# Second engines for four elementwise operations in a list-scheduled attention and feed-forward kernel

## The chip, the cores and the metric

The kernel runs on one core of a Trainium2 chip. The metric is the device time of one execution in microseconds. The engines are called as in the profile: PE is TensorE (matmul), PEld its weight loads, DVE is VectorE, ACT is ScalarE, POOL is GpSimd and SP is SyncE, which issues the DMAs.

## What is computed

Sliding-window attention with a few always visible first keys (sinks), and behind it a feed-forward layer with ELU (batch 4, 8 heads, 768 positions, head dimension 64; 3072 tokens, model width 512, hidden width 2048):

```python
scores = (1 / sqrt(64)) * q @ k.T
keep = (pos_k < n_sink) | ((0 <= pos_q - pos_k) & (pos_q - pos_k < window))   # n_sink 4, window 128
a = softmax(where(keep, scores, -1e9))
x = (a @ v) laid out as 3072 x 512
h = x @ w_in
out = where(h > 0, h, exp(min(h, 0)) - 1) @ w_out
```

Inputs are float32, the two weights float64.

## The kernel before

The 24 tiles of 128 tokens are cut into nine chunks (three of two tiles, six of three). For each chunk `attention` handles four pairs of heads, tile by tile, and `feed_forward` runs over 16 blocks f of 128 hidden units. The first two chunks' blocks come in halves (chunk 0 first half, chunk 1 first half, then the second halves), since meanwhile the 32 weight pieces are still being loaded and converted.

Matmuls run on 16-bit parts (or rounded 32-bit ones for the scores): a value is split into a high half and a low half (value minus high half), and products of the halves are summed in PSUM. So most of the elementwise work makes halves:

- weights (`weights`, `weight_f32`): per piece L292 (ACT), L293 and L294 (DVE, 16-bit shift and mask), L295 (DVE) give a float32 piece wv; L442 (ACT) its high half, L443 (POOL) its low half.
- keys and queries (`split_keys`): L508 (ACT) high, L512 and L514 (POOL) low.
- values (`vtile`): L531 (ACT) high half of V, L532 (DVE) low half, both from the loaded tile vs.
- probabilities, per tile and head: scores (L577, L578; in the first two chunks L584), mask and minimum (L603, DVE), exp (L605, ACT), reciprocal (L609, L610), then L617 (ACT) the scaled high half of probabilities, L618 (DVE) the low half, and for the sinks three small POOL operations (L624, L627, L628). A DMA transpose on the SP queue (L636) turns pq into pt, the values matmul (L650, L655) follows, and L687 (ACT), L688 (DVE) make the halves of x.
- hidden units, per block: 12 matmuls into h (L715); L723 (ACT) g = exp; L725 (DVE) g = (g - 1) times a scale; L726 (DVE) the ELU, max(min(g, 0), h), with h from PSUM, which also frees h's bank; L728 (ACT) the high half gh, L729 (POOL) the low half gl; then the matmuls into acc (L736).

The order is made at build time by `Plan`. Each step is a task with an engine, a duration in us, and dependencies; buffers are rings (`RINGS`), and a writer depends on the users of the buffer some turns earlier. A due time for each task is worked out backward from the matmuls, and a forward pass places tasks: the engine that can start earliest takes its ready task with the earliest due time. A task may have a second way (`or_`: engine, duration, function); it then stands in both engines' queues, and the one that reaches it first takes it:

```python
else:
    while later[e] and later[e][0][0] <= s:
        _, n, t = heapq.heappop(later[e])
        heapq.heappush(now[e], (t.due, n, t))
    ...
    t.take(e)
dur = t.dur
if e == "DVE" and t.slow > 1.0:
    both = min(max(free["POOL"] - s, 0.0), dur * t.slow)
    dur += both * (1.0 - 1.0 / t.slow)
```

With equal start times the engine named first in the order PE, ACT, DVE, POOL, SP takes the task. `slow` stretches a task's planned time on DVE while POOL is planned as busy. Passes backward and forward are repeated eight times, the best modelled end is kept, and every engine then runs its instructions in exactly that order (`keep_order`). No task of the kernel before has a second way.

Of the kernel before, what the change touches and what calls it, by code (L numbers as in the profile page):

```python
# [273 lines left out]
def pool_us(n):  # L274
    return 0.25 + 0.0019 * n
# [73 lines left out]
def fast_path(tc, ctx, first, kq, vx, wt, out, nw, flag):  # L349
# [129 lines left out]
    def attention(c):  # L479
# [12 lines left out]
        def split_keys(h):  # L492


            st = kqs[slot("kqs")]
            buf = kqr[slot("kq")] if c >= WHOLE else None
            o, kw = KQ_OFF[c, h], kc + qc
            if c < WHOLE:
                ld = None
                if (c, h) not in first["kq"]:  # L500
                    ld = add("SP", 0.4, lambda: nc.sync.dma_start(st[:, :kw], kq[:, o : o + kw]), lat=dma_us(P * kw * 4) * 1.15)
                users = []
                return st, None, ld, ld, users
            raw, hi = st[:, :kw], buf[:, :kw]
            ld = None
            if (c, h) not in first["kq"]:
                ld = add("SP", 0.4, lambda: nc.sync.dma_start(raw, kq[:, o : o + kw]), lat=dma_us(P * kw * 4) * 1.15)
            th = add("ACT", act_us(kw), lambda: nc.scalar.activation(hi, raw, AF.Copy), deps=[ld])  # L508

            def low():  # L510
                n = kc if c >= DUP else kw
                nc.gpsimd.tensor_tensor(buf[:, KQ_MAX : KQ_MAX + n] if c >= DUP else buf[:, kw : 2 * kw], raw[:, :n], hi[:, :n].bitcast(F32), ALU.subtract)  # L512
                if c >= DUP:
                    nc.gpsimd.tensor_tensor(hi[D:, kc:], raw[D:, kc:], hi[D:, kc:].bitcast(F32), ALU.subtract)  # L514

            tl = add("POOL", pool_us(kc) + pool_us(qc) if c >= DUP else pool_us(kw), low, deps=[th])
            users = []
            ring("kqs", [ld or th], [th, tl])
            ring("kq", [th], users)
            lo = buf[:, KQ_MAX : KQ_MAX + kc] if c >= DUP else buf[:, kw : 2 * kw]  # L520
            return hi, lo, th, tl, users

        def vtile(g):

            if g not in v_of:
                st, i = vs[slot("vs")], slot("vt")
                ld = None
                if g not in first["vs_"]:
                    ld = add("SP", 0.4, lambda: nc.sync.dma_start(st, vx[:, g * VT : (g + 1) * VT]), lat=dma_us(P * VT * 4))
                hi, lo, users = vh[i], vl[i], []  # L530
                va = add("ACT", act_us(VT), lambda: nc.scalar.activation(hi, st, AF.Copy, scale=V_SCALE), deps=[ld])  # L531
                vb = add("DVE", 0.13 + 0.00108 * VT, lambda: nc.vector.scalar_tensor_tensor(lo, st, V_SCALE, hi, ALU.mult, ALU.subtract), deps=[va], slow=1.35)  # L532
                ring("vs", [ld or va], [va, vb])
                ring("vt", [va], users)
                v_of[g] = hi, lo, va, vb, users
            return v_of[g]

        def sink_rows(b):

            if b not in sk_of:  # L540
                st, sk, users = vs[slot("vs")], sks[slot("sk")], []
                o = SINKS + b * VT
                ld = add("SP", 0.4, lambda: nc.sync.dma_start(st, vx[:, o : o + VT]), lat=dma_us(P * VT * 4))
                va = add("ACT", act_us(VT), lambda: nc.scalar.activation(sk, st, AF.Copy, scale=V_SCALE), deps=[ld])
                vb = add("DVE", 0.13 + 0.00108 * VT, lambda: nc.vector.scalar_tensor_tensor(sk[64:96, :], st[64:96, :], V_SCALE, sk[64:96, :], ALU.mult, ALU.subtract), deps=[va])
                ring("vs", [ld], [va, vb])
                ring("sk", [va], users)
                sk_of[b] = sk, vb, users
            return sk_of[b]

        k = 0
        for p in range(NP):
# [5 lines left out]
            for g in ts:  # L558
# [53 lines left out]
                for e in range(2):  # L612
                    src = e3[:, e, :wd].rearrange("p (b k) -> p b k", k=KW)[:, :, NS:]
                    hi = pq[:, 2 * e * nb : (2 * e + 1) * nb, :]
                    lo = pq[:, (2 * e + 1) * nb : (2 * e + 2) * nb, :]
                    re = rs[:, e : e + 1]
                    a = add("ACT", act_us(nb * P, True), lambda src=src, hi=hi, re=re: nc.scalar.activation(hi, src, AF.Copy, scale=re), deps=[rr])  # L617
                    b = add("DVE", 0.478 if nb == 2 else 0.33, lambda src=src, hi=hi, lo=lo, re=re: nc.vector.scalar_tensor_tensor(lo, src, re, hi, ALU.mult, ALU.subtract), deps=[a], slow=1.5)  # L618
                    parts += [a, b]
                    his.append(a)  # L620
                if t >= 2:

                    def sinks(e3=e3, rs=rs, tmp=tmp, pq=pq):
                        nc.gpsimd.tensor_tensor(tmp, e3[:, :, 0:NS], rs.unsqueeze(2).to_broadcast([P, 2, NS]), ALU.mult)  # L624
                        hi = pq[:, 8, 0:96].rearrange("p (g r) -> p g r", g=3)[:, :, 0 : 2 * NS]
                        flat = tmp.rearrange("p e k -> p (e k)")
                        nc.gpsimd.tensor_copy(hi[:, 0:3:2, :], flat.unsqueeze(1).to_broadcast([P, 2, 2 * NS]))  # L627
                        nc.gpsimd.tensor_tensor(hi[:, 1, :], flat, hi[:, 0, :], ALU.subtract)  # L628

                    b = add("POOL", 0.75, sinks, deps=[rr])  # L630
                    parts.append(b)
                    his.append(b)
                ring("e", [r for r, _ in exps], parts)
# [64 lines left out]
    def feed_forward(c, f0, f1, start):  # L698
# [4 lines left out]
        for f in range(f0, f1):  # L703
            hp = h_ps[slot("h")]
            gf = gs[slot("g")][:, :n]
            i = slot("gh")
            gh, gl = ghs[i], gls[i]

            def stage1(hp=hp, f=f):
                win = w[2 * f].rearrange("p t (a f) -> p t a f", a=ND)  # L710
                k = 0
                for d in range(ND):
                    xh, xl = x[d][:2]
                    for part, xx in ((0, xh), (1, xh), (0, xl)):
                        nc.tensor.matmul(hp[:, :n], win[:, part, d, :], xx[:, :n], start=k == 0, stop=k == 3 * ND - 1)  # L715
                        k += 1

            s1 = add("PE", 12 * (n / 2400 + 0.002), stage1, deps=[v for d in x for v in d[2:4]] + list(w_done[2 * f]), pos=start + 2 * (f - f0))
            for d in x:
                d[4].append(s1)  # L720

            sums = es_of[:, c * NF + f : c * NF + f + 1]
            a = add("ACT", act_us(n) + 0.18, lambda gf=gf, hp=hp, sums=sums: nc.scalar.activation(gf, hp[:, :n], AF.Exp, scale=1.0 / G_SCALE, accum_out=sums), deps=[s1])  # L723
            exps_done.append(a)
            b = add("DVE", 0.14 + 0.00057 * n, lambda gf=gf: nc.vector.tensor_scalar(gf, gf, -1.0, G_SCALE, ALU.add, ALU.mult), deps=[a], slow=2.1)  # L725
            b = add("DVE", dve_us(n), lambda gf=gf, hp=hp: nc.vector.scalar_tensor_tensor(gf, gf, 0.0, hp[:, :n], ALU.min, ALU.max), deps=[b])  # L726
            ring("h", [s1], [b])
            th = add("ACT", act_us(n), lambda gf=gf, gh=gh: nc.scalar.activation(gh[:, :n], gf, AF.Copy), deps=[b])  # L728
            tl = add("POOL", pool_us(n), lambda gl=gl, gf=gf, gh=gh: nc.gpsimd.tensor_tensor(gl[:, :n], gf, gh[:, :n], ALU.subtract), deps=[th])  # L729

            def stage2(order, gl=gl, gh=gh, f=f):
                def run():
                    wout = w[2 * f + 1]
                    for k, i in order:
                        gg, part = ((gh, 0), (gh, 1), (gl, 0))[k]
                        nc.tensor.matmul(acc[i], gg[:, i * P : (i + 1) * P], wout[:, part, :], start=f == f0 and k == 0, stop=f == f1 - 1 and k == 2)  # L736
                return run

            deps = [th, tl, *w_done[2 * f + 1], *(evacs[:nt] if f == f0 else [])]
            at2 = start + 2 * (f - f0) + 1 + 2 * LAG  # L740
            if f < f1 - 1:
                s2 = [add("PE", 3 * nt * 0.215, stage2([(k, i) for k in range(3) for i in range(nt)]), deps=deps, pos=at2)]
            else:

                s2 = [add("PE", 3 * 0.215, stage2([(k, i) for k in range(3)]), deps=deps, pos=at2 + 0.01 * i) for i in range(nt)]
            ring("g", [a], [th, tl])
            ring("gh", [th], s2)
# [307 lines left out]
```

## Time and profile before

| | |
|---|---|
| median of three runs | 658.54 us (656.51 to 658.79) |
| profiled execution, its own time | 656.69 us |
| its span, first to last instruction | 654.8 us |
| mean granted TensorE clock | 0.986 of full speed |
| busy: PE, DVE, ACT, POOL | 610.5, 460.8, 441.8, 332.6 us |

Spans and busy times are those of the one profiled execution. Busy is the time in which at least one instruction of an engine was running. Matmuls overlap in the engine and their ends are modelled, so a busy PE need not be PE at its peak. A time given to an instruction contains what it waited for inside the engine after its start.

### The profile page before, as it was taken

The numbers are of one execution on the slowest core, as the hardware profiler recorded it, in microseconds if no ns is written. First come the engines' busy times: TensorE is split into PE (matmuls) and PEld (weight loads), VectorE is DVE, ScalarE is ACT, GpSimd is POOL, SyncE is SP. The second block draws the span as 40 slices with busy tenths as digits, with TensorE's granted clock in tenths as the row PEclk, the third lists the DMA queues.
The fourth block names the chain that finished last, engine by engine and source line by source line (L and its number), as shares of the span: only waits on it lengthen the run. The fifth ranks groups of instructions, "written<-read, shape, count | busy, mean of one in ns | idle before, by whom it ended". The sixth has DMA issues, their size and how long they took to land.

```text
span 654.8 us, 13359 instructions
## 1 busy us (share of the span) xinstructions
PE 610.5 (93%) x4449; PEld 369.6 (56%) x4449; DVE 460.8 (70%) x1243; ACT 441.8 (67%) x1300; POOL 332.6 (51%) x497
## 2 busy tenths in 40 slices
PE   3786799699999999999999999999999999999995
PEld 1453466466776565655555555565555556555552
DVE  6989979987866777568677877668677776533222
ACT  4988778878877777667667776677667766523231
POOL 0166968795656665535445655544445654212221
PEclk9998889999999999999999999999999999999998
DMA  7889974766746554346444766565654733301001
GB/s 280 212 214 305 259 239 161 222 167 171 190 110 132 148 149 108 90 125 180 123 105 95 197 150 124 78 145 140 145 101 102 200 84 90 75 27 48 1 0 54
DMA packets 125500, 90.78 MB, mean 139 GB/s; under 512 B 104304, under 2 KB 104304, under 8 KB 125424
## 3 DMA queue, kind: packets, MB, share of 16 engines
q1 hardware_dynamic: 125424, 89.85, 52.9%
q8 instruction: 37, 0.61, 0.4%
q14 instruction: 39, 0.32, 0.1%
HBM read 57.32 MB, written 7.34 MB: 99 GB/s over the span
## 4 chain that ended last, share of the span: by engine, by line
PE 80%; DVE 8%; issue 4%; POOL 3%; ACT 2%; DMA 2%; SPq 0%; DVEq 0%; POOLq 0%; ACTq 0%
PE h L715 35%; PE acc L736 34%; PE po L650 4%; PE s L577 3%; PE s L578 3%; DVE wv L295 2%; POOL w L443 1%; DVE wu L294 1%; DMA pt<-pq 1%; DVE wu L293 1%; DVE e L603 1%; POOL gl L729 1%; DVE pq L618 1%; POOL kq L512 1%; PE s L584 1%
## 5 line engine op out<-in xcount | busy, mean ns | idle before, releaser
L715 PE MATMUL h<-x,w 128*128 128x384 f16 (+1 forms) x1728 | 278.4, 312 | 7.4 <-DVE g L726 5.6
L715 PEld LDWEIGHTS <-w 128*128 128x128 f16 x1728 | 166.4, 99 | 102.2 <-issue 4.9
L729 POOL TENSOR_TENSOR gl<-g,gh 128x384 f16<-128x384 f32 (+1 forms) x144 | 128.2, 891 | 179.7 <-ACT gh L728 145.6
L736 PE MATMUL acc<-w,gh 128*128 128x512 f16 x768 | 193.4, 381 | 0.0
L725 DVE TENSOR_SCALAR g<-g 128x384 f32<-128x384 f32 (+1 forms) x144 | 70.5, 489 | 104.9 <-ACT g L723 104.3
L723 ACT ACTIVATE g<-h 128x384 f32<-128x384 f32 (+1 forms) x144 | 65.2, 453 | 98.3 <-PE h L715 90.3
L618 DVE SCALAR_TENSOR_TENSOR pq<-e,st,pq 128x256 f16<-128x256 f32 (+1 forms) x192 | 111.3, 611 | 16.0 <-ACT pq L617 15.1
L736 PEld LDWEIGHTS <-gh 128*128 128x128 f16 x768 | 70.3, 98 | 69.7 <-issue 1.1
L736 PE MATMUL acc<-w,gl 128*128 128x512 f16 x384 | 109.2, 379 | 0.1
L603 DVE CUSTOM_DVE_ANT_0 e<-s,m 128x264 f32<-128x264 f32 (+1 forms) x192 | 71.7, 404 | 46.5 <-PE s L578 40.8
L605 ACT ACTIVATE e<-e,st 128x264 f32<-128x264 f32 (+1 forms) x192 | 93.1, 486 | 9.5 <-DVE st L603 8.6
L617 ACT ACTIVATE pq<-e,st 128x256 f16<-128x256 f32 (+1 forms) x192 | 85.0, 480 | 15.8 <-DVE st L610 13.6
L728 ACT ACTIVATE gh<-g 128x384 f16<-128x384 f32 (+1 forms) x144 | 69.3, 481 | 34.7 <-DVE g L726 33.3
L512 POOL TENSOR_TENSOR kq<-kqs,kq 128x396 fp32r<-128x396 f32 (+1 forms) x56 | 67.7, 1209 | 38.0 <-ACT kq L508 37.8
L726 DVE SCALAR_TENSOR_TENSOR g<-g,h 128x384 f32<-128x384 f32 (+1 forms) x144 | 72.7, 505 | 1.5
L736 PEld LDWEIGHTS <-gl 128*128 128x128 f16 x384 | 37.6, 98 | 45.9 <-POOL gl L729 0.6
L508 ACT ACTIVATE kq<-kqs 128x780 fp32r<-128x780 f32 (+2 forms) x56 | 49.0, 878 | 20.2 <-PE s L578 16.8
L577 PE MATMUL s<-kq 128*128 128x264 f32 x160 | 55.2, 363 | 6.1 <-DVE st L603 2.9
L443 POOL TENSOR_TENSOR w<-wv,w 128x512 f16<-128x512 f32 x32 | 38.8, 1215 | 39.4 <-ACT w L442 25.7
L514 POOL TENSOR_TENSOR kq<-kqs,kq 64x384 fp32r<-64x384 f32 (+1 forms) x56 | 55.7, 995 | 4.4
L650 PE MATMUL po<-pt,vh 128*64 128x128 f16 x704 | 42.0, 231 | 8.4 <-DMA pt<-pq 6.7
L650 PEld LDWEIGHTS <-vh 128*64 128x64 f16 x704 | 30.1, 115 | 22.5 <-issue 16.0
(79 smaller groups left out, 604.1 us busy)
## 6 DMA issues: line engine op xcount, KB each, us to landing
raw<-in_wt_dram SPq DMA_DIRECT2D x32, 512.0 KB, 5.6
kqs<-in_kq_dram SPq DMA_DIRECT2D x24, 456.0 KB, 3.5
kqs<-in_kq_dram SPq DMA_DIRECT2D x24, 390.0 KB, 3.7
vs<-in_vx_dram SPq DMA_DIRECT2D x28, 256.0 KB, 3.1
out_dram<-wv SPq DMA_DIRECT2D x24, 256.0 KB, 3.6
vm<-in_vx_dram SPq DMA_DIRECT2D x6, 768.0 KB, 4.8
kqs<-in_kq_dram SPq DMA_DIRECT2D x12, 326.0 KB, 3.6
pt<-pq SPq DMA_TRANSPOSE x96, 3.2
```

The lines of the kernel that those rows point to most:

```text
L512: nc.gpsimd.tensor_tensor(buf[:, KQ_MAX : KQ_MAX + n] if c >= DUP else buf[:, kw : 2 * kw], raw[:, :n], hi[:, :n].bitcast(F32), ALU.subtract)
L577: nc.tensor.matmul(sp[:, :wd], q, hi[:, c0 : c0 + wd], start=True, stop=False)
L603: red = add("DVE", 0.24 + 0.001 * wd, lambda ee=ee, me=me, sp=sps[e], m=m, wd=wd: nc.vector.tensor_tensor_reduce(ee, sp[:, :wd], m[:, :wd] ...
L605: ex = add("ACT", 0.47 + 0.00085 * wd, lambda ee=ee, me=me, rs=rs[:, e : e + 1]: nc.scalar.activation(ee, ee, AF.Exp, bias=me, scale=-1.0, ...
L617: a = add("ACT", act_us(nb * P, True), lambda src=src, hi=hi, re=re: nc.scalar.activation(hi, src, AF.Copy, scale=re), deps=[rr])
L618: b = add("DVE", 0.478 if nb == 2 else 0.33, lambda src=src, hi=hi, lo=lo, re=re: nc.vector.scalar_tensor_tensor(lo, src, re, hi, ALU.mult ...
L650: nc.tensor.matmul(po[e * D : (e + 1) * D, oc], vts[i][x][:, vo : vo + D], pt[:, (2 * e + part) * nb + i, :], start=new, stop=last)
L715: nc.tensor.matmul(hp[:, :n], win[:, part, d, :], xx[:, :n], start=k == 0, stop=k == 3 * ND - 1)
L725: b = add("DVE", 0.14 + 0.00057 * n, lambda gf=gf: nc.vector.tensor_scalar(gf, gf, -1.0, G_SCALE, ALU.add, ALU.mult), deps=[a], slow=2.1)
L726: b = add("DVE", dve_us(n), lambda gf=gf, hp=hp: nc.vector.scalar_tensor_tensor(gf, gf, 0.0, hp[:, :n], ALU.min, ALU.max), deps=[b])
L729: tl = add("POOL", pool_us(n), lambda gl=gl, gf=gf, gh=gh: nc.gpsimd.tensor_tensor(gl[:, :n], gf, gh[:, :n], ALU.subtract), deps=[th])
L736: nc.tensor.matmul(acc[i], gg[:, i * P : (i + 1) * P], wout[:, part, :], start=f == f0 and k == 0, stop=f == f1 - 1 and k == 2)
```

## The change

Four tasks get a second way: the ELU's exp - 1 step (L725) may run on POOL, the low half of V (L532) may run on POOL as two operations (scale, then subtract), the scaled high half of probabilities (L617) may run on POOL, and the high half of g (L728) may run on DVE. Three planned durations are raised (low half of the keys by 1.12, the sinks from 0.75 to 1.0, and the stretch of V's low half from 1.35 to 1.5). A function `low` is also defined in `sink_rows`, where nothing uses it.

```diff
-            tl = add("POOL", pool_us(kc) + pool_us(qc) if c >= DUP else pool_us(kw), low, deps=[th])
+            tl = add("POOL", 1.12 * (pool_us(kc) + pool_us(qc)) if c >= DUP else pool_us(kw), low, deps=[th])
...
-                vb = add("DVE", 0.13 + 0.00108 * VT, lambda: nc.vector.scalar_tensor_tensor(lo, st, V_SCALE, hi, ALU.mult, ALU.subtract), deps=[va], slow=1.35)
+                def low():
+                    nc.gpsimd.tensor_scalar(st, st, V_SCALE, None, ALU.mult)
+                    nc.gpsimd.tensor_tensor(lo, st, hi, ALU.subtract)
+
+                vb = add("DVE", 0.13 + 0.00108 * VT, lambda: nc.vector.scalar_tensor_tensor(lo, st, V_SCALE, hi, ALU.mult, ALU.subtract), deps=[va], slow=1.5, or_=("POOL", 1.95, low))
...
-                    a = add("ACT", act_us(nb * P, True), lambda src=src, hi=hi, re=re: nc.scalar.activation(hi, src, AF.Copy, scale=re), deps=[rr])
+                    a = add("ACT", act_us(nb * P, True), lambda src=src, hi=hi, re=re: nc.scalar.activation(hi, src, AF.Copy, scale=re), deps=[rr], or_=("POOL", 0.25 + 0.00088 * nb * P, lambda src=src, hi=hi, re=re: nc.gpsimd.tensor_scalar(hi, src, re, None, ALU.mult)))
...
-                    b = add("POOL", 0.75, sinks, deps=[rr])
+                    b = add("POOL", 1.0, sinks, deps=[rr])
...
-            b = add("DVE", 0.14 + 0.00057 * n, lambda gf=gf: nc.vector.tensor_scalar(gf, gf, -1.0, G_SCALE, ALU.add, ALU.mult), deps=[a], slow=2.1)
+            b = add("DVE", 0.14 + 0.00057 * n, lambda gf=gf: nc.vector.tensor_scalar(gf, gf, -1.0, G_SCALE, ALU.add, ALU.mult), deps=[a], slow=2.1, or_=("POOL", 0.25 + 0.00088 * n, lambda gf=gf: nc.gpsimd.tensor_scalar(gf, gf, -1.0, G_SCALE, ALU.add, ALU.mult)))
...
-            th = add("ACT", act_us(n), lambda gf=gf, gh=gh: nc.scalar.activation(gh[:, :n], gf, AF.Copy), deps=[b])
+            th = add("ACT", act_us(n), lambda gf=gf, gh=gh: nc.scalar.activation(gh[:, :n], gf, AF.Copy), deps=[b], slow=2.1, or_=("DVE", 0.14 + 0.00057 * n, lambda gf=gf, gh=gh: nc.vector.tensor_copy(gh[:, :n], gf)))
```

## Rows read from the trace of the kernel before

**Rows 1.** The page: TensorE's busy tenths in 40 equal slices of the span.

```profile
PE   3786799699999999999999999999999999999995
```

**Rows 2.** Stretches: us, busy us per engine (instructions), granted clock, DMA share, GB/s.

```profile
16.00:49.00 33.00, 25.73 (x174) 16.12 (x175) 29.55 (x103) 28.98 (x92) 12.62 (x21) 1.00 0.87 213
...
49.00:98.00 49.00, 37.38 (x316) 24.26 (x314) 44.66 (x102) 39.79 (x112) 35.25 (x50) 0.86 0.94 268
...
98.00:131.00 33.00, 27.94 (x209) 18.56 (x207) 33.00 (x66) 27.62 (x72) 25.21 (x31) 1.00 0.61 193
...
16.00:131.00 115.00, 91.06 (x695) 58.94 (x696) 107.21 (x269) 96.38 (x275) 73.08 (x100) 0.94 0.82 231
...
180.00:620.00 440.00, 438.99 (x3197) 260.20 (x3196) 293.69 (x783) 290.30 (x853) 216.59 (x323) 1.00 0.47 114
```

**Rows 3.** Groups, 16 to 131 us, VectorE: busy us, mean ns | idle before.

```profile
L293 DVE TENSOR_SCALAR wu<-raw 128x512 uint16<-128x512 uint16 x30 | 21.7, 722 | 0.0
...
L295 DVE SCALAR_TENSOR_TENSOR wv<-acc,wu 128x512 int32<-128x512 int32 x30 | 20.4, 681 | 1.2 <-ACT acc L292 1.0
...
L294 DVE TENSOR_SCALAR wu<-raw 128x512 uint16<-128x512 uint16 x30 | 19.9, 664 | 0.0
...
L618 DVE SCALAR_TENSOR_TENSOR pq<-e,st,pq 128x256 f16<-128x256 f32 x31 | 16.2, 550 | 1.6 <-ACT pq L617 1.3
...
L725 DVE TENSOR_SCALAR g<-g 128x256 f32<-128x256 f32 x21 | 11.1, 528 | 4.3 <-ACT g L723 4.3
...
L726 DVE SCALAR_TENSOR_TENSOR g<-g,h 128x256 f32<-128x256 f32 x21 | 8.5, 406 | 0.0
...
L532 DVE SCALAR_TENSOR_TENSOR vl<-vs,vh 128x512 f16<-128x512 f32 x4 | 4.1, 1042 | 0.0
```

**Rows 4.** Groups, 16 to 131 us, GpSimd.

```profile
L443 POOL TENSOR_TENSOR w<-wv,w 128x512 f16<-128x512 f32 x30 | 36.2, 1208 | 39.0 <-ACT w L442 25.3 <-DVE x L688 10.1 <-DVE g L726 1.9
```

**Rows 5.** The chain of waits, 98 to 131 us, shares by line.

```profile
by line: issue 23.6%; DVE wv L295 14.7%; POOL w L443 12.1%; DVE wu L294 11.4%; DVE wu L293 9.9%; DVE g L725 7.5%; DVE pq L618 5.2%; POOL gl L729 4.6%; ACT w L442 3.5%; DVE g L726 3.0%; ACT acc L292 2.1%; DVE e L603 2.1%; ACT g L723 1.4%; DV
```

**Rows 6.** In order of time: start us, us, engine, line, operation.

```profile
48.93 0.88 DVE L618 SCALAR_TENSOR_TENSOR pq<-e,st,pq 128x256 f16<-128x256 f32 x2
...
53.44 0.45 DVE L293 TENSOR_SCALAR wu<-raw 128x512 uint16<-128x512 uint16 x1
...
54.11 0.28 DVE L725 TENSOR_SCALAR g<-g 128x256 f32<-128x256 f32 x1
...
56.17 0.67 POOL L729 TENSOR_TENSOR gl<-g,gh 128x256 f16<-128x256 f32 x1 [3.21 <-ACT gh L728]
...
56.80 1.16 POOL L443 TENSOR_TENSOR w<-wv,w 128x512 f16<-128x512 f32 x1
...
56.94 1.34 DVE L293 TENSOR_SCALAR wu<-raw 128x512 uint16<-128x512 uint16 x1
...
85.09 0.20 POOL L627 CAST pq<-st 128x16 f16<-128x16 f32 x1
...
302.91 0.91 POOL L729 TENSOR_TENSOR gl<-g,gh 128x384 f16<-128x384 f32 x1 [1.70 <-ACT gh L728]
...
306.90 0.68 DVE L532 SCALAR_TENSOR_TENSOR vl<-vs,vh 128x512 f16<-128x512 f32 x1
...
310.07 0.49 ACT L723 ACTIVATE g<-h 128x384 f32<-128x384 f32 x1 [0.17 <-PE h L715]
```

**Rows 7.** Groups, 16 to 49 us, ScalarE.

```profile
L617 ACT ACTIVATE pq<-e,st 128x256 f16<-128x256 f32 (+1 forms) x20 | 8.2, 464 | 1.5 <-DMA pt<-pq 1.3
```

**Rows 8.** Groups, 49 to 98 us, VectorE.

```profile
L725 DVE TENSOR_SCALAR g<-g 128x256 f32<-128x256 f32 x10 | 5.3, 528 | 3.1 <-ACT g L723 3.1
...
L532 DVE SCALAR_TENSOR_TENSOR vl<-vs,vh 128x512 f16<-128x512 f32 x3 | 3.4, 1162 | 0.0
```

**Rows 9.** Groups, 98 to 131 us, VectorE.

```profile
L725 DVE TENSOR_SCALAR g<-g 128x256 f32<-128x256 f32 x9 | 5.0, 555 | 0.0
```

**Rows 10.** Waits, 16 to 131 us, TensorE: us in total, times, longest.

```profile
PE h L715 <- DVE g L726: 5.6, 5, 2.5
```

More of the change, by code (lines that the diff above doesn't have):

```diff
@@ L544, in sink_rows, with low @@
                 va = add("ACT", act_us(VT), lambda: nc.scalar.activation(sk, st, AF.Copy, scale=V_SCALE), deps=[ld])
+                def low():
+                    nc.gpsimd.tensor_scalar(st, st, V_SCALE, None, ALU.mult)
+                    nc.gpsimd.tensor_tensor(lo, st, hi, ALU.subtract)
                 vb = add("DVE", 0.13 + 0.00108 * VT, lambda: nc.vector.scalar_tensor_tensor(sk[64:96, :], st[64:96, :], V_SCALE, sk[64:96, :], ALU.mult, ALU.subtract), deps=[va])
```

## The prediction

> **What bounds the kernel now.** I read the profile from the whole to the part. First the page: TensorE's line of 40 slices has digits under 9 only among the first eight and in the last one [rows 1]. The table by stretch shows the same in microseconds [rows 2]. From 180 to 620 us PE is busy 439.0 of 440 us: there nothing that VectorE, ScalarE or GpSimd does faster can be gained, only lost. From 16 to 131 us PE is busy 91.1 of 115, so 23.9 us are idle, and between 49 and 98 us the granted clock is 0.86, a mix of its two levels (2.4 and 1.2 GHz) after PE stood idle for 7.3 of the 33 us before; that costs another 49 x 0.14 = 6.9 us of TensorE time. So the change can be worth at most about 31 us, all of it before 131 us; the first 16 us (loads, masks) and the tail hold none of the edited work to speak of.
>
> What holds PE in that stretch? DVE is busy 107.2 of 115 us, ACT 96.4, POOL 73.1 [rows 2]. The groups say with what [rows 3, 4]: 30 weight pieces cost DVE three operations each (L293, L294, L295: 722, 664 and 681 ns), ACT two and POOL one of 1208 ns, beside the attention of the first chunks and the first ELUs. The chain of waits from 98 to 131 us runs over DVE and POOL lines, hardly over PE [rows 5]. So it is three elementwise engines, VectorE ahead, that set the pace.
>
> A second thing is to be seen in the order of time [rows 6]. L293 takes 0.45 us at 53.44, when POOL stands still, but 1.34 at 56.94, when POOL has started L443 at 56.80: it ends after L443 does. L725 takes 0.28 us at 54.11, with POOL idle, and 528 ns in the mean [rows 3]; L618 0.44 (two in 0.88) and 550, L532 0.68 and 1042. So these DVE operations (L293, L294, L725, and L532 and L618 with two inputs in SBUF) and POOL's operations exclude each other, and DVE's mean times carry that wait.
>
> **The change, part by part.** Each option goes to whichever engine comes free first in the plan, so I work out how many move.
>
> *Price of a one-input GpSimd operation.* No row shows one of this size. Above it is the two-input one: 0.67 us at 256 columns and 1.16 at 512 [rows 6], so 1.9 ns a column over 0.18 fixed. Below it is a 16-column cast, 0.20 us [rows 6]. I take half the slope for half the inputs: 0.18 + 0.25 = 0.43 us at 256 columns, 0.67 at 512; ends 0.20 and 0.67. The V low half takes two operations on GpSimd, 0.67 + 1.16 = 1.83 us, against 0.68 on a free DVE.
>
> *What one us more of POOL costs DVE.* From 16 to 131 us DVE's exclusive operations took longer in the mean than alone [rows 3, 6]: L293 30 x (0.72 - 0.45) = 8.2, L294 (as L293 alone) 30 x (0.66 - 0.45) = 6.4, L618 31 x (0.55 - 0.44) = 3.4, L725 21 x (0.53 - 0.28) = 5.2, L532 4 x (1.04 - 0.68) = 1.4, together 24.6 us beside 73.1 us of POOL. That is 0.34 us of DVE for each us of POOL.
>
> *16 to 49 us.* POOL is idle 20 of 33 us; ACT and DVE are busy 29.0 and 29.6 [rows 2]. Of the 20 probability high halves (L617, 464 ns [rows 7]) I let 8 move: ACT is rid of 3.7 us. The step itself is no shorter (0.43 for about 0.5), and DVE, unrelieved, comes next, so of these 3.7 I count 1.5; ends 0 and 3.7.
>
> *49 to 98 us.* DVE always has a queue; POOL is idle 28% of the time and otherwise frees about as often as DVE, so some 6 of 10 L725 and 2 of 3 L532 move [rows 8]: 6 x 0.53 + 2 x 1.16 = 5.5 us off DVE. To POOL come 6 x 0.43 + 2 x 1.83 + 4 L617 x 0.43 = 8.0 us, which cost DVE 8.0 x 0.34 = 2.7. Net 2.8. If all the idle time went, the clock would give back 6.9 us; 2.8 of 11.6 us idle is a quarter, 1.7 us. With both ends of the price POOL gets 4.7 or 11.3 us, and the net is 3.9 or 1.7.
>
> *98 to 131 us.* Of nine L725 some 4 move [rows 9], 2.2 us off DVE, 1.7 onto POOL, which cost 0.6: net 1.6. But here POOL is on the chain itself (L443 12.1%, L729 4.6% [rows 5]), and the 1.7 us delay it, so I count 0.5; ends -1.7 and 1.6.
>
> *gh on DVE* (L728): nothing before 131 us, where DVE is the fuller of the two. *After 131 us* I cost all moves at nothing: PE's own 439 of 440 us hide them. The cover can be read off: a gl ends at 302.91 + 0.91 = 303.82, and its two-deep buffer of g is not written again before 310.07 [rows 6], the matmuls that read gl coming later still; 6.2 us take in a -1 on POOL and several two-input operations ahead of it. Without that cover each late gl would cost PE its lateness. *The raised costs* (key low half, sinks, V low half) issue nothing and only reorder; zero, with the reshuffling of a whole plan as an unknown of some 3 us either way.
>
> *The new wait.* L726 now waits on POOL where the -1 moved. DVE runs in order, so L293 to L295, L603 and L618 stand behind it, and behind them the weight pieces and the next scores; PE already waits 5.6 us for L726 to free the bank [rows 10]. POOL's queue in front of a -1 can be a 1.2 us L443. The planner knows both engines' queues but not that POOL is held up by DVE.
>
> *Sum.* 1.5 + 2.8 + 1.7 + 0.5 = 6.5 us off the profiled execution's 656.69 gives 650.2. That execution lies 1.85 us below the median of the three runs, 658.54; a new program's median may lie anywhere in such a spread, and I say **651**.
>
> **The rule of the skill that speaks against it.** The row first: L293 waited until POOL's L443 was over and only then ran [rows 6]. The Trainium skill, page SBUF — State Buffer, section Who interferes with whom, says that VectorE's two-port modes, and its operations with two SBUF inputs against GpSimd's reads, contend for one port pair which the first comer holds for its whole instruction. By that rule all four options only add holding time, also the one that relieves ScalarE, which is the first rival below. The trace agrees with it: 1.34 us for 0.45 [rows 6].
>
> **The rivals.**
> *The shared path becomes the bound; slower.* From 16 to 131 us POOL is busy 73.1 us, and DVE's exclusive operations, alone, would take 60 x 0.45 + 31 x 0.44 + 21 x 0.28 + 4 x 0.68 = 49.2 [rows 3, 6]: together 122 in 115 us, which fits only because recorded times overlap at their ends. The moves add 10 x (0.43 - 0.28) + 2 x (1.83 - 0.68) + 13 x 0.43 = 9.4 us of exclusive time up to 131 us, the last term for work that ScalarE did without holding anybody up. Half of it on the path gives 661, all of it 666; 664. It decides where that sum is over the stretch's length. For it: from 98 to 131 us DVE is busy 33.0 of 33 us and POOL 25.2. Against it: from 16 to 49 us POOL is busy only 12.6 of 33 [rows 2].
> *The engines level out.* DVE, ACT and POOL together are busy 276.7 of 345 engine-us, 92 each. If DVE came down from 107 to 92, that is 15 us, and with it half the clock's loss, 3 us: 639. Against it: the exclusion, and that dependent chains never fill three engines.
> *Nothing that counts.* POOL takes few, or what DVE saves it waits: 656.7 less or plus the few us of a reshuffled plan, 655 to 661. For it: the net in each stretch is 1 to 3 us.
>
> **How the numbers follow.** The forecast, with its own range of 646 to 655 (gains between the ends of the parts): 0.40. Level engines: 0.15. Nothing: 0.20. Shared path: 0.25. About 0.5% (3.3 us) is what a measurement of this kernel can tell from no change. So faster 0.55, same 0.20, slower 0.25. The range of 8 in 10 takes in the centres of both outer rivals: 638 to 664.
>
> **What would show it.** Right: one-input GpSimd rows at L725's place of about 0.43 us; before 131 us DVE busy some 5 us less, POOL 12 or so more; PE idle from 16 to 131 us some 5 us less than 23.9; the granted clock from 49 to 98 us above 0.86; 180 to 620 us still full. Wrong: L293 and L618 longer than 722 and 550 ns in the mean, so that DVE stays as busy with less work; new PE waits for POOL's w and gl or for L726; or PE idle after 180 us. The prediction falls if a one-input GpSimd operation takes as long as a two-input one, or if the new order, not the moves, decides where PE waits.

## The result, and the profile after

The changed kernel takes 666.65 us (median of four runs, 664.90 to 667.78) beside 658.66 before: ratio 1.0126, 95% interval 1.0092 to 1.0161. It is slower by about 8 us, above the range of the prediction (638 to 664).

The code after has eight lines more from V's low half on, so L617 became L625, L618 L626, L725 L733, L726 L734, L728 L736 and L729 L737; V's low half on GpSimd is L533 and L534. The page's line of 40 slices for TensorE:

```profile
PE   3686689889999999999999999999999999999995
```

The dent is where it was [rows 1], and now reaches into the ninth slice. The stretches say where the time went (columns as in [rows 2]: busy us of PE, PEld, DVE, ACT, POOL, then the granted clock):

```profile
16.00:49.00 33.00, 24.42 (x156) 15.41 (x155) 28.66 (x99) 27.45 (x89) 18.56 (x23) 1.00 0.82 213
49.00:98.00 49.00, 33.55 (x261) 20.90 (x261) 44.90 (x93) 36.37 (x102) 44.55 (x65) 0.86 0.76 227
98.00:131.00 33.00, 32.02 (x262) 21.42 (x260) 31.04 (x57) 26.92 (x73) 30.40 (x39) 1.00 0.81 246
16.00:131.00 115.00, 89.98 (x676) 57.73 (x675) 104.60 (x247) 90.74 (x262) 93.51 (x125) 0.94 0.79 228
131.00:180.00 49.00, 44.60 (x337) 30.51 (x338) 42.74 (x108) 36.89 (x113) 43.02 (x61) 0.97 0.59 158
180.00:620.00 440.00, 438.62 (x3232) 261.93 (x3230) 292.51 (x792) 276.91 (x814) 276.44 (x393) 1.00 0.49 117
```

From 180 to 620 us hardly anything changed (438.6 of 440 busy, 439.0 before). From 16 to 131 us PE is idle for 25.0 us instead of 23.9, and from 131 to 180 us for 4.4 instead of 1.0, with the clock at 0.97 there (1.00 before). POOL is busy 93.5 us instead of 73.1 up to 131 us, and from 49 to 98 us 44.6 of 49; DVE, which was to be relieved, 104.6 instead of 107.2. And it got less done: 27 weight pieces up to 131 us where it had been 30. VectorE's groups from 16 to 131 us, beside [rows 3]:

```profile
L626 DVE SCALAR_TENSOR_TENSOR pq<-e,st,pq 128x256 f16<-128x256 f32 x32 | 21.9, 712 | 2.1 <-ACT pq L625 1.2 <-POOL pq L625 0.7
L293 DVE TENSOR_SCALAR wu<-raw 128x512 uint16<-128x512 uint16 x27 | 21.1, 780 | 0.7 <-DMA raw<-in_wt_dram 0.7
L294 DVE TENSOR_SCALAR wu<-raw 128x512 uint16<-128x512 uint16 x28 | 20.6, 735 | 0.0
...
L733 DVE TENSOR_SCALAR g<-g 128x256 f32<-128x256 f32 x6 | 3.1, 524 | 0.8 <-ACT g L731 0.8
```

Only 6 of about 20 exp - 1 are left on DVE, and no tile of V. But the shift and the mask take 780 and 735 ns (722 and 664 before), the probabilities' low half 712 (550 before). GpSimd's groups of the same stretch:

```profile
L443 POOL TENSOR_TENSOR w<-wv,w 128x512 f16<-128x512 f32 x27 | 33.5, 1245 | 6.0 <-ACT w L442 3.6 <-DVE st L611 1.7 <-POOL kq L514 0.5
...
L533 POOL TENSOR_SCALAR vs<-vs 128x512 f32<-128x512 f32 x5 | 8.0, 1595 | 0.4
...
L733 POOL TENSOR_SCALAR g<-g 128x256 f32<-128x256 f32 x14 | 6.9, 494 | 5.7 <-ACT st L617 3.0 <-ACT g L731 2.7
L534 POOL TENSOR_TENSOR vl<-vs,vh 128x512 f16<-128x512 f32 x5 | 5.8, 1168 | 0.4
...
L625 POOL TENSOR_SCALAR pq<-e,st 128x256 f16<-128x256 f32 x3 | 3.2, 1067 | 4.2 <-DVE st L618 4.2
```

L733, the moved exp - 1, takes 494 ns. But L533, the scale of V, takes 1595, and L625, the probabilities, 1067; the plan had 0.48 us for the probabilities, and for both operations of V 1.95 us, where they now take 2.76. One place where it can be seen, in the order of time, first POOL, then PE (in brackets the idle time before, and who ended it):

```profile
79.52 1.49 POOL L533 TENSOR_SCALAR vs<-vs 128x512 f32<-128x512 f32 x1
81.09 1.16 POOL L534 TENSOR_TENSOR vl<-vs,vh 128x512 f16<-128x512 f32 x1
82.20 1.34 POOL L443 TENSOR_TENSOR w<-wv,w 128x512 f16<-128x512 f32 x1
```

```profile
83.60 1.89 PE L723 MATMUL h<-x,w 128*128 128x256 f16 x11 [2.51 <-POOL w L443]
```

A V tile holds POOL from 79.5 to 82.2 us; the weights' low half L443 stands behind it, and PE waits 2.5 us for that. In the table of waits from 16 to 180 us this one was 1.5 us before (first line), when PE waited longer for L726 [rows 10]; now it leads the list (second line):

```profile
PE h L715 <- POOL w L443: 1.5, 3, 1.0
...
PE h L723 <- POOL w L443: 10.8, 6, 2.9
```

The weights as a whole come later, too. The last of their 32 low halves, before and after:

```profile
139.69 1.29 POOL L443 TENSOR_TENSOR w<-wv,w 128x512 f16<-128x512 f32 x1 [0.41 <-ACT w L442]
...
150.85 1.16 POOL L443 TENSOR_TENSOR w<-wv,w 128x512 f16<-128x512 f32 x1
```

### The profile page after: what moved, and what is told of

Read it like the earlier page. It is cut to its first block, busy times and chain, and to the rows that moved or that the text cites. A ratio compares the mean times of both kernels' runs of the same rounds, so it can differ in the third digit from the quotient of the medians.

```text
span 663.1 us, 13326 instructions
## 1 busy us (share of the span) xinstructions
PE 614.4 (93%) x4449; PEld 371.5 (56%) x4449; DVE 460.5 (69%) x1216; ACT 420.7 (63%) x1233; POOL 428.4 (65%) x607
## 4 chain that ended last, share of the span: by engine, by line
PE 79%; POOL 7%; DVE 6%; DMA 3%; issue 3%; ACT 1%; SPq 0%; POOLq 0%; DVEq 0%; ACTq 0%
PE h L723 34%; PE acc L744 33%; PE po L658 4%; PE s L585 3%; PE s L586 3%; POOL w L443 2%; DMA raw<-in_wt_dram 1%; POOL gl L737 1%; DMA pt<-pq 1%; DVE pq L626 1%; PE s L592 1%; DVE e L611 1%; DVE wv L295 1%; POOL vs L533 1%; DMA words<-in_window_dram 1%
## 5 line engine op out<-in xcount | busy, mean ns | idle before, releaser
L737 POOL TENSOR_TENSOR gl<-g,gh 128x384 f16<-128x384 f32 (+1 forms) x144 | 127.7, 887 | 132.5 <-ACT gh L736 82.7
L733 DVE TENSOR_SCALAR g<-g 128x384 f32<-128x384 f32 (+1 forms) x99 | 57.2, 577 | 107.8 <-ACT g L731 107.6
L626 DVE SCALAR_TENSOR_TENSOR pq<-e,st,pq 128x256 f16<-128x256 f32 (+1 forms) x192 | 114.1, 619 | 15.1 <-ACT pq L625 12.0
L625 ACT ACTIVATE pq<-e,st 128x256 f16<-128x256 f32 (+1 forms) x159 | 71.3, 484 | 19.9 <-DVE st L618 19.2
L736 ACT ACTIVATE gh<-g 128x384 f16<-128x384 f32 (+1 forms) x110 | 53.7, 488 | 43.1 <-DVE g L734 41.6
L512 POOL TENSOR_TENSOR kq<-kqs,kq 128x396 fp32r<-128x396 f32 (+1 forms) x56 | 66.2, 1182 | 19.2 <-ACT kq L508 19.2
L734 DVE SCALAR_TENSOR_TENSOR g<-g,h 128x384 f32<-128x384 f32 (+1 forms) x144 | 72.6, 504 | 8.5 <-POOL g L733 7.3
L585 PE MATMUL s<-kq 128*128 128x264 f32 x160 | 55.5, 366 | 8.1 <-DVE st L611 5.9
L443 POOL TENSOR_TENSOR w<-wv,w 128x512 f16<-128x512 f32 x32 | 39.4, 1239 | 6.0 <-ACT w L442 3.6
L586 PE MATMUL s<-kq 128*128 128x264 f32 x160 | 42.3, 282 | 0.0
```

What stands on the lines that cost most here:

```text
L585: nc.tensor.matmul(sp[:, :wd], q, hi[:, c0 : c0 + wd], start=True, stop=False)
```

## The experiments

Theory M: the moved GpSimd operations are dearer than the plan and I assumed. Theory S: the path that VectorE and GpSimd share makes them long, and VectorE with them. Theory O: it is the new order. Every ratio is to the kernel before on the same chip, with its 95% interval.

**The operations by themselves (`prices`).** Each form six times, VectorE idle (one line of each loop; four more forms are left out):

```diff
+nc.gpsimd.tensor_scalar(st, st, 1.0, None, ALU.mult)              # L1015, L1017 at 256 columns
+nc.gpsimd.tensor_scalar(st, st, 0.0, 1.0, ALU.add, ALU.mult)      # L1019, L1021 at 256 columns
+nc.gpsimd.tensor_scalar(h2, src, re, None, ALU.mult)              # L1025, re: one value per partition
+nc.gpsimd.tensor_scalar(h2, src, re, 1.0, ALU.mult, ALU.mult)     # L1027
+nc.gpsimd.tensor_tensor(lo, st, hv, ALU.subtract)                 # L1033
```

> This kernel computes nothing of the reference: it runs the GpSimd operations of the change by themselves, six of each form, with VectorE idle, and writes a tile of anything to the output. Theory M (the operations are simply longer than planned): a one-operation scale of 512 columns takes 1.45 to 1.55 us also here, a pointer-scaled 256 columns into 16 bits 0.85 to 0.95, and the two-operation exp - 1 form 0.4 to 0.5 at 256. Theory S (they are long in the changed kernel because VectorE holds them up): here they take about 0.7, 0.45 and 0.4.

GpSimd's groups:

```profile
L1015 POOL TENSOR_SCALAR st<-st 128x512 f32<-128x512 f32 x6 | 9.0, 1492 | 4.2 <-DVE rs L1010 4.2
L1033 POOL TENSOR_TENSOR lo<-st,hv 128x512 f16<-128x512 f32 x6 | 6.9, 1152 | 0.5
L1025 POOL TENSOR_SCALAR hv<-e,rs 128x256 f16<-128x256 f32 x6 | 5.6, 927 | 0.0
L1017 POOL TENSOR_SCALAR st<-st 128x256 f32<-128x256 f32 x6 | 5.2, 861 | 0.0
...
L1019 POOL TENSOR_SCALAR st<-st 128x512 f32<-128x512 f32 x6 | 3.7, 620 | 0.4
...
L1027 POOL TENSOR_SCALAR hv<-e,rs 128x256 f16<-128x256 f32 x6 | 3.0, 493 | 0.0
...
L1021 POOL TENSOR_SCALAR st<-st 128x256 f32<-128x256 f32 x6 | 2.4, 404 | 0.5
```

Theory M holds as to the durations: they are close to what the trace of the changed kernel shows, with nobody else running. What makes the difference is the form: with one operation a `tensor_scalar` takes 1492 ns at 512 columns, with two operations 620; with the scale from a pointer 927 and 493. Exp - 1 has two operations, and V and the probabilities had one.

**The plan is told the true prices (`true_costs`); only the cheap two moves (`exp_gh_only`); the order with the old engines (`order_kept_engines_back`).**

```diff
# true_costs
-or_=("POOL", 1.95, low)
+or_=("POOL", 2.8, low)
-or_=("POOL", 0.25 + 0.00088 * nb * P, lambda src=src, ...
+or_=("POOL", 0.29 + 0.0026 * nb * P, lambda src=src, ...
-or_=("POOL", 0.25 + 0.00088 * n, lambda gf=gf: nc.gpsimd...
+or_=("POOL", 0.40 + 0.0003 * n, lambda gf=gf: nc.gpsimd...
# exp_gh_only: the or_ of V's low half and of the probabilities taken out
# order_kept_engines_back, at the end of Plan.order
-            t.take(e)
+            t.take(next(iter(t.ways)))
```

> The four options stay, but the plan is told the durations seen in the changed kernel's trace: V low half on GpSimd 2.8 us instead of 1.95, probabilities 0.29 + 0.0026 a column (0.96 for 0.48), exp - 1 0.40 + 0.0003 a column. Theory M: the plan moves fewer of the dear ones, weights come in time, PE's waits for the weights' low half fall from 10 us to under 4, and the time is 652 to 659. Theory S: what moves still holds VectorE up; 660 to 666. Theory O (any new order is some per cent off): anything from 652 to 670, without relation to those waits.

> Only exp - 1 and the high half of g may move; V's low half and the probabilities stay on VectorE and ScalarE; the three raised costs stay. Theory M: the two dear moves are gone and the two cheap ones stay, so 650 to 658, with waits for the weights' low half under 4 us. Theory S: exp - 1 on GpSimd costs VectorE what it saves, 656 to 662. Theory O: no relation.

> The plan is that of the changed kernel, order and all, but when the instructions are written out every task goes back to its first engine. So the order of the changed kernel is run with the engines of the kernel before. Theory M: the slow GpSimd operations are gone, so GpSimd runs ahead of its plan, while VectorE and ScalarE get work that the order left no room for: 656 to 664. Theory S: the same direction, at most 660. Theory O (the order itself is bad): 664 to 672.

Measured: 668.10 us, ratio 1.0146 (1.0115 to 1.0177); 658.10, 0.9998 (0.9977 to 1.0019); 663.59, 1.0082 (1.0060 to 1.0103). The second lies where M and S meet, the third at the edge of M and O. The first fell outside what M and S expected (only O's wide range holds it), and the trace says why M was wrong in it:

```profile
L533 POOL TENSOR_SCALAR vs<-vs 128x512 f32<-128x512 f32 x17 | 26.8, 1579 | 18.9 <-ACT vh L531 18.0
...
L625 POOL TENSOR_SCALAR pq<-e,st 128x256 f16<-128x256 f32 x21 | 20.0, 954 | 6.8 <-POOL kq L514 5.1 <-DVE st L618 0.9 <-DMA pt<-pq 0.7
...
L625 POOL TENSOR_SCALAR pq<-e,st 128x128 f16<-128x128 f32 x11 | 6.8, 622 | 4.5 <-DVE st L618 3.4 <-PE acc L744 0.8 <-PE s L586 0.4
```

17 V tiles still move (16 in the changed kernel) and 32 probability tiles (33). The plan gives a task to the engine that is free first, whatever it costs there: the true price hardly changed the choice. PE's waits for the weights' low half, which theory M put under 4 us in the first two runs, were 9.4 and 7.4 us. The third shows that the order, run with the old engines, is worse than the old order; in it PE's scores wait for DVE to empty their banks (2.4 and 3.1 us from 16 to 180 us in the kernel before):

```profile
PE s L585 <- DVE st L611: 9.0, 6, 2.7
PE s L592 <- DVE st L611: 7.4, 9, 2.4
```

Over all, PE is idle no longer than before from 16 to 131 us (22.5 us for 23.9). It is idle longer from 131 to 180 us, 4.5 us for 1.0, and the granted clock is lower, 0.83 for 0.86 from 49 to 98 us and 0.93 for 1.00 from 131 to 180:

```profile
49.00:98.00 49.00, 34.52 (x260) 21.92 (x261) 45.84 (x101) 37.13 (x102) 36.21 (x53) 0.83 0.79 230
...
131.00:180.00 49.00, 44.54 (x332) 30.75 (x333) 38.23 (x106) 38.55 (x121) 32.22 (x47) 0.93 0.58 146
```

**The cheap form (`two_op_forms`, `v_two_op`).** The plan stays as it is, instruction for instruction; a neutral second operation is added, to both scales or to V's alone:

```diff
-                    nc.gpsimd.tensor_scalar(st, st, V_SCALE, None, ALU.mult)
+                    nc.gpsimd.tensor_scalar(st, st, V_SCALE, 1.0, ALU.mult, ALU.mult)
...
-nc.gpsimd.tensor_scalar(hi, src, re, None, ALU.mult)
+nc.gpsimd.tensor_scalar(hi, src, re, 1.0, ALU.mult, ALU.mult)
```

> The plan of the changed kernel, instruction for instruction. Only the form of two GpSimd operations changes: the scale of V and the scaling of the probabilities are written with a second, neutral operation (times 1.0), which by itself took 620 ns for 1492 at 512 columns and 493 for 927 at 256. These are the durations that the plan assumes. Theory M (price): 12 to 15 us of GpSimd time go before 131 us, the waits for the weights' low half fall from 10 us to under 4, and the time is 654 to 660. Theory O (the order): with the moves nearly free the order remains, which with the old engines took 663.6; 661 to 665.

> The plan of the changed kernel; only the scale of V is written in the two-operation form (0.7 us for 1.6), the probabilities stay in the dear form. It divides the 6.5 us that both forms together gave back. Theory M: five V tiles before 131 us at 0.9 us each against five probability tiles at 0.3 to 0.45, so about two thirds is V's: 661 to 664. If the probabilities' form were the dear part: 664 to 667.

Measured: 660.16, 1.0040 (1.0027 to 1.0052), and 661.70, 1.0058 (1.0038 to 1.0079). So of the 1.26% the two forms are 0.86, V's 0.68 and the probabilities' 0.18; the 0.18 is less than the two intervals can separate. What is left is 0.4%.

The time came out just above what theory M expected, and two of its signs did not come. From 16 to 131 us GpSimd is busy only 3.3 us less (90.2 for 93.5), not 12 to 15, and PE's waits for the weights' low half did not fall under 4 us:

```profile
PE h L723 <- POOL w L443: 9.8, 8, 2.0
```

At the place shown above (PE at 83.60 us in the changed kernel), PE still waits, 1.9 us for 2.5:

```profile
79.71 2.53 PE L723 MATMUL h<-x,w 128*128 128x256 f16 x11 [1.86 <-POOL w L443]
```

Both runs have the same matmuls in the same order, so they can be compared matmul by matmul. Of the 5.0 us by which the cheap forms' run is ahead at the end, 2.9 are there at the matmul that starts at 39.59 us in the changed kernel and at 36.74 here, behind a wait for the probabilities' transpose. The lead is 2.0 us from 100 to 130 us and 3.7 at 180. So a good part of the price was lost before 40 us, ahead of the place shown:

```profile
39.59 0.32 PE L658 MATMUL po<-pt,vh 128*64 128x128 f16 x2 [1.59 <-DMA pt<-pq]
...
36.74 0.32 PE L658 MATMUL po<-pt,vh 128*64 128x128 f16 x2
```

VectorE and GpSimd from 16 to 131 us:

```profile
L626 DVE SCALAR_TENSOR_TENSOR pq<-e,st,pq 128x256 f16<-128x256 f32 x32 | 22.5, 728 | 1.2 <-ACT pq L625 0.8 <-POOL pq L625 0.3
L294 DVE TENSOR_SCALAR wu<-raw 128x512 uint16<-128x512 uint16 x28 | 21.8, 777 | 0.0
...
L293 DVE TENSOR_SCALAR wu<-raw 128x512 uint16<-128x512 uint16 x28 | 19.5, 698 | 0.0
```

```profile
16.00:131.00 115.00, 90.87 (x688) 58.65 (x689) 105.42 (x250) 91.09 (x265) 90.19 (x128) 0.94 0.86 234
```

The scale of V is now 0.7 us, but DVE's exclusive operations are as long as in the changed kernel: 32 x (0.728 - 0.44) + 28 x (0.777 - 0.45) + 28 x (0.698 - 0.45) = 25.3 us, with six L733 and three casts 28, beside 90.2 us of POOL: 0.31 us per us, where I had 0.34 from the kernel before (the casts' time alone, 0.3 us, is an estimate). That part of theory S is right: DVE is busy 105.4 us for 107.2 before, with fewer operations of its own. The Trainium skill (page SBUF — State Buffer, section Who interferes with whom) says that a VectorE instruction in a two-port mode and a GpSimd instruction block each other for the whole instruction, whichever comes first. The longer means here agree with it (777 and 698 ns for 450 alone); the single case is in [rows 6].

**Costs alone, a nudge, and the moves alone (`costs_only`, `before_nudged`, `order_before_engines_moved`).**

```diff
# costs_only: all four or_ taken out of the changed kernel
# before_nudged
-    HOP = {"PE": 0.15, "ACT": 0.08, "DVE": 0.08, "POOL": 0.2, "SP": 0.0}
+    HOP = {"PE": 0.15, "ACT": 0.081, "DVE": 0.081, "POOL": 0.2, "SP": 0.0}
# order_before_engines_moved: the plan of before; MOVED lists the changed kernel's 128 moved tasks
             t.take(e)
             t.start = s
+            if t.n in MOVED:
+                t.eng, t.dur, t.fn = t.second
```

> No second ways; only the raised planned costs, so a new order with the old engines. Theory O in its strong form (any new order costs some tenths of a per cent): 655 to 668, most likely above 658. Theory M: nothing is dear here, 656 to 661.

> The kernel before with one planning constant moved by a nanosecond (the planned hop from ScalarE and VectorE, 0.080 to 0.081 us), which has no meaning and only gives another order. Theory O: such a plan is as far from the kernel before as the change's order was, 650 to 668, beyond 1% with a chance of a third. Theory M: within 0.5%, 655 to 662.

> The order of the kernel before; the 128 tasks that the changed kernel runs on a second engine are put there when the instructions are written out, with the same operations. So the moves are run without the new order. Theory M: the dear GpSimd operations stand in an order that left no room for them, 663 to 675. Theory O: the moves alone are harmless, 656 to 661.

Measured: 656.55, 0.9980 (0.9969 to 0.9991); 658.14, 0.9999 (0.9983 to 1.0014); 690.05, 1.0488 (1.0463 to 1.0513). The nudge left the orders of TensorE, ScalarE and GpSimd as they were and exchanged a few VectorE instructions behind 370 us, so it says nothing of other orders. The last is 32 us slower, more than either theory expected: the moved operations stand in queues that were not planned for them, and PE waits, 11.5 us for GpSimd's low half of the keys alone, even far from the start:

```profile
16.00:131.00 115.00, 83.54 (x623) 53.92 (x622) 90.43 (x235) 85.15 (x249) 83.54 (x117) 0.91 0.76 209
...
180.00:620.00 440.00, 428.89 (x3210) 257.94 (x3208) 300.68 (x808) 274.03 (x826) 275.25 (x400) 1.00 0.48 121
```

**Which moves cost, in plans of their own (`two_op_no_v`, `two_op_no_pq`, `finish_rule`).** Cheap forms; one `or_` taken out, or a task left to the engine that would finish it earlier:

```diff
# finish_rule, in Plan.forward
-                    if not t.done:
-                        break
+                    if t.done:
+                        continue
+                    other = [max(free[o], ready[t]) + d for o, (d, _) in t.ways.items() if o != e]
+                    if other and not t.left and min(other) < s + t.ways[e][0]:
+                        t.left = True
+                        t = None
+                    break
```

> Cheap forms, and V's low half may not move at all (it is 0.68 us alone on VectorE, 1.86 on GpSimd). Theory Q (what is left of the loss is GpSimd's queue: weights' low halves behind moved work): fewer waits for the weights' low half than the 9.8 us with both cheap forms, 655 to 659. Theory O (the order): no relation, 655 to 664.

> Cheap form for V, and the probabilities may not move. Theory Q: less is taken from GpSimd's queue than without V, 657 to 661. Theory O: no relation, 655 to 664.

> Cheap forms, and another rule in the plan: an engine leaves a task with two ways to the other engine when that one would finish it earlier (by the times at which both come free), so price counts in the choice and not only who is free first. Theory Q: fewer moves, the weights' low halves in time, 653 to 657, under the kernel before. Theory O: no relation, 655 to 664.

Measured: 659.38, 1.0024 (1.0007 to 1.0040); 656.33, 0.9969 (0.9951 to 0.9987); 660.89, 1.0045 (1.0031 to 1.0059). The first came out just above its range of theory Q, the second under its own. The rule by finish is a miss; it moved no V tile, but 73 high halves of g went to DVE where the changed kernel had 34. It seemed that the probabilities' moves cost some 0.5% even in the cheap form; the next runs tested that.

**The same in one order (`pq_back`, `v_back`, `exp_back`), and a plan with two moves (`v_exp_only`).** `two_op_forms` with one kind of move put back when the instructions are written out:

```diff
-            t.take(e)
+            t.take(next(iter(t.ways)) if list(t.ways) == ["ACT", "POOL"] else e)   # pq_back
```

> The changed kernel's order with the cheap forms (660.2), and the 33 moved probability tiles run on ScalarE again. Theory Q (their time in GpSimd's queue delays the weights' low halves): 656 to 659, with fewer waits for those. Theory R (the order was made for them, and it is the order that costs): 660 to 663.

> The changed kernel's order with the cheap forms, and the 16 moved V low halves run on VectorE again (0.68 us for 1.86). Theory Q: 657 to 660. Theory R (VectorE has no room for them in this order): 661 to 664.

> The changed kernel's order with the cheap forms, and the 45 moved exp - 1 run on VectorE again. Theory Q: GpSimd loses 6 us before 131 us, VectorE gets as much, 658 to 662. Theory R: 661 to 664.

> A plan of its own: cheap form, only V's low half and exp - 1 may move. Theory Q: without the probabilities the weights are in time, 654 to 658, under the kernel before. Theory R (each new order its own chance): 655 to 663.

Measured: 660.93, 1.0044 (1.0027 to 1.0060); 659.43, 1.0029 (1.0015 to 1.0043); 662.61, 1.0070 (1.0053 to 1.0086); 659.21, 1.0027 (1.0012 to 1.0041). Beside 1.0040 with all cheap moves, the probabilities' moves cost nothing (theory Q falls for them), V's perhaps 0.1%, which is inside the intervals, and exp - 1 on GpSimd gains 0.3% in this order. PE's waits for the weights' low half fell from 9.8 us to 7.1, 5.2 and 6.4, and the time did not follow. The plan with two moves missed theory Q's range.

**The best version again (`two_op_no_pq_again`, `costs_only_again`).**

> The cheap form for V, second ways for V's low half, exp - 1 and the high half of g, none for the probabilities; measured again with more rounds. If the cheap moves are worth something in themselves: 655.5 to 657 and at least 0.1% under the raised costs alone. If it is the order that each plan happens to give: within 0.15% of them, or above.

> Only the raised planned costs, no second ways, measured again with more rounds: 656 to 657.5, some 0.2% under the kernel before, if the first measurement holds.

Measured: 655.69, 0.9963 (0.9949 to 0.9977), and 657.11, 0.9973 (0.9962 to 0.9985). Both are faster than both kernels, by a little; the 0.1% between them lies inside the intervals, so whether the moves themselves gain is not told apart from the order.

## Why the prediction was wrong, step by step

**What bounds the kernel** held in the main: what changed lies before 180 us, and PE's 439 of 440 us behind it took the moves with 0.4 us of loss. But I put all moves after 131 us at nothing and showed the cover only from 180 us on. From 131 to 180 us PE's idle time rose by 3.4 us, more than the 1.1 from 16 to 131, and the clock fell from 1.00 to 0.97. The cover behind 180 us holds only where the order was planned for the moves; in the order of before, the same moves let PE stand idle for 11 of these 440 us.

**The price of a one-input operation is the first step that failed.** "I take half the slope for half the inputs", 0.43 us at 256 columns and 0.67 at 512, with 0.67 as the upper end at 256. Measured alone: 0.86 to 0.93 and 1.49, above the upper end, for the one-operation form, and 0.40 and 0.62 for the two-operation form. The number of inputs was the wrong measure, and my own condition ("if a one-input GpSimd operation takes as long as a two-input one") came true: 1.49 us beside 1.15 for the subtraction. Exp - 1 was priced right (0.43; 0.49 in the kernel), the V low half at 1.83 instead of 2.76 (1.595 + 1.168). With the forms cheap and all else fixed, 0.86 of the 1.26% go.

**The gain is the other step, and the larger one.** I forecast a gain of 6.5 us, 1.0%, and the kernel lost 1.26%: 2.3 points apart. The price is 0.9 of them. The other 1.4 are the gain that did not come even with the cheap forms: these took 0.48 to 0.73 us in the trace, near the price that I had assumed, and the kernel was still 0.40% slower. Up to 98 us I charged GpSimd's added work only with what it costs VectorE, and with nothing for the old work that stands behind it. With the cheap forms, from 16 to 131 us, GpSimd is busy 90.2 us for 73.1, DVE 105.4 for 107.2 with 28 weight pieces done for 30, and PE is idle 24.1 us for 23.9, where I had expected some 5 less. PE's wait for L726 went (5.6 us before, 0.4 now), and that for L443 came in its place (9.8 for 1.5). Which of these makes the 0.40% is not shown, since in the runs with one move put back that wait fell without the time.

**How many move** was off as well, and made the price count for more. I let 2 V and 8 + 4 probability tiles move before 131 us. The trace of after has 5 V tiles from 16 to 131 us and two before, and 5 probability tiles from 16 to 131; 14 exp - 1 moved where I had 10. So the dearest move came more than three times as often as I thought, and the planner did not mind: it asks who is free, not who is done first.

**What POOL costs DVE**, 0.34 us per us, was right as a mean (0.31 with the cheap forms; of what was added, 3.4 us for 17.1, it is 0.20), and so was the sign that I named for the wrong case: L293 and L618 longer, DVE as busy with less work.

**16 to 49 us and 49 to 98 us** were to gain 1.5, and 2.8 with 1.7 of the clock: PE's idle time there rose from 7.3 to 8.6 and from 11.6 to 15.5, and the clock from 49 to 98 us stayed at 0.86. **98 to 131 us** did gain (PE busy 32.0 for 27.9 us), but at that time PE was making up work that it had missed. The 6.9 us that I gave to the clock between 49 and 98 us were too many, since they count idle time too: PE was busy for 10.9 of the 13.7 us at the lower level (56.0 to 59.4, 66.3 to 69.7 and 79.9 to 86.8 us), which is some 5.4 us, an estimate.

**Rearranging**, "some 3 us either way", was too small where the plan has second ways: the changed kernel's order with its old engines is 0.82% or 5.4 us slower. This need not be the price of an order in itself, since that order had no room for what was put back; with the cheap moves in it 0.40% are left.

**The rivals.** The shared path, 661 to 666, had the side and came near the size, but its reckoning was made with my price too (and with 13 probability tiles, where the parts have 12). With the cheap forms the same instructions in the same order lie 0.4% above before, where it asked for 0.7% to 1.4%. Nor is the price a longer wait of VectorE: over L293, L294 and the probabilities' low half that wait is 25.6 us with the dear forms and 25.3 with the cheap ones. But dear GpSimd time is time on the shared path as well, and the runs do not exclude that path for the 0.40% that are left. With the cheap forms the time is within the rival "nothing that counts", 655 to 661.

Open: why one plan with second ways and cheap forms comes out at 0.9963 and another at 1.0045. The six plans with second ways and no dear form spread over that range, and with the order fixed, neither the probabilities' nor V's moves made that difference. One thing goes with it: the time at which the last low half of the weights starts. In the eight other profiled traces where that is by 144.1 us (139.7 before), the ratios are 0.9963 to 1.0027; in the ten where it is 144.9 us or later (150.9 in the changed kernel), they are 1.0029 to 1.0488. The order run with the old engines is among the late ones, at 151.0 us, with nothing moved to GpSimd. No run changed the weights' time alone, so it is not shown to be the cause, and it does not set the size (one plan at 139.7 us has 1.0027).

## What to carry to other kernels

Before an elementwise operation is given to GpSimd, time exactly that form alone: a neutral second operation made it about two times faster here, and one run of 77 us would have shown it. A list scheduler that hands a task to whoever is free first did not get better by true prices here. An engine that gets moved work is a queue for what already stands there, so put a price on that wait too; a cheap operation alone did not make the moves pay. And look at when the work that everything needs, here the weights, is done, whichever engine holds it up.

## What the hardware showed that I had not expected

GpSimd's `tensor_scalar` with one operation takes 1492 ns at 512 columns and 861 at 256, 2.5 ns a column, more than a subtraction of two tensors (1152 ns at 512); with two operations it takes 620 and 404, 0.8 ns a column. A scale from a pointer with 16-bit output is the same: 927 against 493 ns at 256 columns.
